# Attention, then two gated matrix layers on one core: spent attention tiles handed to the weights one at a time, a first part in 256 columns, key tiles at the end of the memory, and another issue order

## The chip, the cores and the metric

The kernel runs on one core of one Trainium2 chip. A core has TensorE (PE in the rows; PEld is its weight load), VectorE (DVE), ScalarE (ACT), GpSimd (POOL), SyncE (SP, which here issues every transfer) and 16 DMA engines. The metric is the device time of one execution in microseconds (us), the median of the runs.

## The reference, cut to what matters

```python
# q, k, v: 2 x 8 heads x 768 x 64, float32; scale = 1/8
k_sum = k in blocks of 32 tokens, max;  v_sum = v in blocks of 32, mean   # 24 blocks
scores = concat(scale*q@k.T where |i-j| < 16, scale*q@k_sum.T + log(32))
x = softmax(scores) @ concat(v, v_sum)            # -> 1536 tokens x 512
h = x @ w_in1;  x = (h * clip(h + 3, 0, 6) / 6) @ w_out1   # 512 -> 2048 -> 512
h = x @ w_in2;  x = (h * sigmoid(h)) @ w_out2              # 512 -> 2048 -> 512
```

## The kernel before

**Attention.** 24 units u, each 64 query tokens of one batch with all 8 heads. `load` brings q, k and v in parts of 256 tokens (batch 0's keys, values and first queries into `stage` tiles, the rest into two `qkv` buffers, in two pieces with 64-element runs for q and k), `tr` transposes them on PE (L470), `k_copy`, `q_copy` and `k_max` take them out of PSUM. For a unit come `keys` (POOL), `scores` (PE, L575), `masked` (DVE), `exps` (ACT), `normal` (POOL), `turn` (PE, a transpose, L632), `turned`, and `mix` (PE, L644), whose result `mixed_hi`/`mixed_lo` write as a rounded part and a rest into the input tile x. A mix needs its batch's block sums of v, so all of that batch's v: `v_sums` (PE, L519), `v_add` (DVE) and `v_rows` (PE, L538).

**The layers.** Every operand of a layer is a rounded `float32r` tile (hi) and a rest (lo), and a product is three matmuls (hi·hi, hi·lo, lo·hi). A layer runs in two halves of 8 blocks f of 128 hidden channels, each over three chunks of 512 tokens (tiles x0, x1 and `x_late`). A step i = (layer, half, chunk, f) is `hidden i` (12 matmuls, L682), `act i` (ACT), `gate i` (DVE), `gate_hi i` (ACT or DVE), `gate_lo i` (DVE, L711) and `project i` (12 matmuls in two parts, L732 and L735) into four PSUM banks that a chunk keeps over its 8 steps. There are 96 steps, all 512 columns wide.

**Weights.** 64 pieces h of 512 KB pass through `fetch` (SP), `conv_mag` (ACT), `conv_low`, `conv_clamp`, `conv_join`, `conv_sign` (DVE: rounding to hi), `conv_hi` (DVE or ACT) and `conv_lo` (DVE or POOL, L420). Two pieces fill one weight tile of 8 KB per partition. Eight weight tiles exist at first; four more (`we`), three `gw` and two `rw` tiles come at `end_attention`, when a memory pool with all attention tiles closes; until then there are two `gn` tiles and one `rn`.

**Memory.** Tiles lie behind one another in the order of allocation. Per partition these are: constants 2,144 bytes, x0 and x1 16,384 each, the two key tiles kT (tags ka0, ka1) 12,608 each, and then tiles whose sizes are all multiples of 2,048: `mag`, `bits`, `words`, the weights, the tile `late` (attention's units first, `x_late` afterwards), then the attention pool.

**Order.** `ORDER` is a table written ahead: each engine runs its instructions in that order and waits by semaphores; a star puts an operation on DVE.

Of the kernel before, what the change touches and what calls it, by code (L numbers as in the profile page):

```python
# [78 lines left out]
zero, rouse 0, rouse 1, rouse 2, rouse 3, rouse 4, rouse 5, load k 0 2, table 0, par k 2 1, par k 2 0, tr k 0  # L79
2 0, k_max 0 2 0, k_copy 0 2 0*, tr k 0 2 1, load k 0 0, par k 0 1, par k 0 0, tr k 0 0 1, k_max 0 2 1, k_copy  # L80
0 0 1*, tr k 0 0 0, k_copy 0 0 0*, k_max 0 0 0, load q 0 0, par q 0 0, fetch 0, conv_low 0, par q 0 1, k_copy
0 2 1, clear, tr q 0 0 1, q_copy 0 0 1 1, q_copy 0 0 1 0*, load k 0 1, par k 1 0, conv_mag 0, par k 1 1,
conv_clamp 0, conv_join 0, tr q 0 0 0, q_copy 0 0 0 0, tr k 0 1 1, tr k 0 1 0, k_copy 0 1 0, k_max 0 1 1, load
k 1 1, tr k 1 1 1, k_copy 0 1 1, k_max 0 1 0, k_max 0 0 1, keys 0, k_copy 1 1 1, k_max 1 1 1, keys 3,
conv_sign 0, table 1, tr k 1 1 0, k_max 1 1 0, q_copy 0 0 0 1, scores 0, masked 0, conv_hi 0, exps 0, load k 1
0, tr k 1 0 0, k_max 1 0 0, fetch 1, conv_low 1, conv_mag 1, tr k 1 0 1, keys 1, scores 1, masked 1,
conv_clamp 1, conv_join 1, exps 1, conv_sign 1, guard 0, inverse 0, keys 2, k_copy 1 0 1, guard 1, scores 3,
masked 3, inverse 1, load k 1 2, tr k 1 2 1, tr k 1 2 0, k_max 1 2 0, k_copy 1 0 0, k_copy 1 2 0, load q 0 1,
exps 3, scores 2, masked 2, k_max 1 2 1, guard 3, tr q 0 1 1, q_copy 0 1 1 0, tr q 0 1 0, q_copy 0 1 0 0*,
q_copy 0 1 1 1*, normal 0, turn 0, load v 0 0, normal 1, keys 4, turn 1, k_max 1 0 1, q_copy 0 1 0 1, k_copy 1  # L90
1 0*, v_sums 0 0, v_add 0 0, scores 4, masked 4, keys 7, scores 7, conv_lo 0, exps 2, guard 2, inverse 2,
inverse 3, exps 4, guard 4, conv_hi 1*, load q 0 2, turned 0*, tr q 0 2 0, q_copy 0 2 0 0*, tr q 0 2 1, q_copy
0 2 1 1, q_copy 0 2 0 1, load q 1 0, keys 5, scores 5, inverse 4, tr q 1 0 1, keys 6, turned 1, masked 5, exps
# [824 lines left out]
```

## Time and profile before

| | |
|---|---|
| median of 3 runs | 627.41 us (625.96 to 627.69) |
| the profiled execution, its own time | 626.98 us |
| its span, first to last instruction | 625.2 us |
| granted TensorE clock, mean | 0.989 |
| PE / DVE / ACT / POOL busy, share of the span | 97% / 64% / 39% / 10% |
| last matmul ends | about 622 us |

The span is 1.8 us under that execution's time, and the execution 0.4 us under the median. Matmuls overlap, so PE's busy share says little of its pace; the distance from one matmul's start to the next does.

### The profile page before, as it was taken

The page shows a single profiled execution, that of the slowest core. Times are in us where ns is not written, and L with a number is a line of the kernel's source. Part 1 is how long each engine was busy: PE and PEld are TensorE (multiplying, and loading weights), DVE is VectorE, ACT ScalarE, POOL GpSimd, SP SyncE. Part 2 cuts the span into 40 slices and gives each one's busy share as a digit, 9 for nine tenths or more (in the row PEclk, how much of TensorE's full clock was granted, in tenths as well). Part 3 has the DMA queues.
Part 4 walks back from the last instruction along what each step waited for, and adds up shares of the span by engine and source line. Part 5 has one row for each costly group of instructions (what it writes and reads, how often), then busy time and mean ns, then how long its engine had stood idle before and what let it go on. Part 6 is the DMA issues. An engine that isn't in the chain of part 4 may idle for free.

```text
span 625.2 us, 8645 instructions
## 1 busy us (share of the span) xinstructions
PE 608.6 (97%) x3208; PEld 500.3 (80%) x3208; DVE 398.8 (64%) x908; ACT 243.4 (39%) x568; POOL 63.4 (10%) x90
## 2 busy tenths in 40 slices
PE   6899999999999989999999999999999999999997
PEld 5788788888788868888888888888888888888886
DVE  5789999856569999862369999432159423332442
ACT  3789787454235454331143453211243221111100
POOL 3576443111010000000000000000000000000000
PEclk8799999999999998999999999999999999999999
...
GB/s 240 208 225 179 226 158 141 80 60 26 92 67 135 143 161 136 150 17 1 1 0 102 139 107 128 66 0 1 0 1 101 1 1 1 68 0 1 68 1 67
DMA packets 69051, 51.56 MB, mean 82 GB/s; under 512 B 36369, under 2 KB 63505, under 8 KB 69009
## 3 DMA queue, kind: packets, MB, share of 16 engines
...
q8 instruction: 25, 0.41, 0.3%
...
## 4 chain that ended last, share of the span: by engine, by line
PE 82%; DVE 13%; ACT 3%; issue 1%; POOL 0%; ACTq 0%; DVEq 0%
PE bank L682 37%; PE bank L735 21%; PE bank L732 18%; DVE bits L398 2%; DVE bits L405 2%; PE bank L575 2%; PE bank L644 1%; DVE bits L385 1%; DVE mag L392 1%; PE bank L632 1%; PE bank L470 1%; ACT prob L604 1%; DVE rw L700 1%; DVE gw L711 1%; PE bank L851 1%
## 5 line engine op out<-in xcount | busy, mean ns | idle before, releaser
L682 PE MATMUL bank<-x,w 128*128 128x512 f32 x720 | 179.2, 396 | 0.7 <-DVE x L667 0.7
L682 PEld LDWEIGHTS bank<-x,w 128*128 128x128 f32 x720 | 133.7, 188 | 30.9 <-ACT early_units L604 0.9
L735 PE MATMUL bank<-w,gw 128*128 128x512 f32 (+1 forms) x456 | 103.8, 378 | 0.0
L735 PEld LDWEIGHTS bank<-w,gw 128*128 128x128 f32 x456 | 82.9, 188 | 16.8
L711 DVE TENSOR_TENSOR gw<-rw,gw 128x512 fp32r<-128x512 f32 x80 | 55.1, 689 | 49.2 <-ACT gw L707 47.5
L704 DVE TENSOR_TENSOR rw<-bank,rw 128x512 f32<-128x512 f32 x48 | 32.9, 686 | 69.3 <-ACT rw L695 69.3
L380 ACT ACTIVATE mag<-words 128x512 f32<-128x512 f32 x64 | 43.3, 676 | 65.4 <-DVE bits L398 65.2
L695 ACT ACTIVATE rw<-bank 128x512 f32<-128x512 f32 x48 | 28.4, 595 | 93.6 <-PE bank L682 84.8
L682 PE MATMUL bank<-x,we 128*128 128x512 f32 x240 | 59.0, 393 | 0.0
L732 PE MATMUL bank<-gw,w 128*128 128x512 f32 x240 | 58.0, 390 | 0.0
L707 ACT CAST gw<-rw 128x512 fp32r<-128x512 f32 x45 | 28.0, 622 | 71.1 <-PE bank L735 43.4
L682 PEld LDWEIGHTS bank<-x,we 128*128 128x128 f32 x240 | 45.0, 188 | 10.3
L732 PEld LDWEIGHTS bank<-gw,w 128*128 128x128 f32 x240 | 45.1, 188 | 9.6
L732 PE MATMUL bank<-gn,w 128*128 128x512 f32 x192 | 48.4, 398 | 0.2 <-DVE gn L711 0.2
L398 DVE SCALAR_TENSOR_TENSOR bits<-mag,bits 128x512 uint32<-128x512 uint32 x64 | 45.0, 703 | 0.9
L405 DVE SCALAR_TENSOR_TENSOR bits<-words,bits 128x512 uint32<-128x512 uint32 x64 | 45.0, 703 | 0.4
L732 PEld LDWEIGHTS bank<-gn,w 128*128 128x128 f32 x192 | 35.1, 188 | 8.2 <-DVE gn L711 0.5
L700 DVE SCALAR_TENSOR_TENSOR rw<-rw,bank 128x512 f32<-128x512 f32 x32 | 21.8, 682 | 28.7 <-ACT rw L693 28.7
L732 PE MATMUL bank<-gw,we 128*128 128x512 f32 x144 | 37.6, 406 | 2.4 <-DVE gw L711 0.9
L732 PEld LDWEIGHTS bank<-gw,we 128*128 128x128 f32 x144 | 27.9, 196 | 10.0 <-DVE gw L711 1.7
L735 PE MATMUL bank<-we,gw 128*128 128x512 f32 x144 | 34.7, 390 | 0.0
L682 PE MATMUL bank<-x_late,w 128*128 128x512 f32 x144 | 34.1, 389 | 0.0
...
## 6 DMA issues: line engine op xcount, KB each, us to landing
words<-in_moe_w_in_dram SPq DMA_DIRECT2D x32, 512.0 KB, 3.8
words<-in_moe_w_out_dram SPq DMA_DIRECT2D x32, 512.0 KB, 3.4
...
out_dram<-acc SPq DMA_DIRECT2D x11, 256.0 KB, 2.0
qkv<-in_q_dram SPq DMA_DIRECT2D x10, 256.0 KB, 5.1
stage<-in_k_dram SPq DMA_DIRECT2D x3, 512.0 KB, 5.4
qkv<-in_k_dram SPq DMA_DIRECT2D x6, 256.0 KB, 4.7
stage<-in_v_dram SPq DMA_DIRECT2D x3, 512.0 KB, 6.8
```

What stands on the lines that cost most here:

```text
L380: nc.scalar.activation(out=out, in_=low_high(h)[:, 1].bitcast(F32), func=AF.Abs, scale=EXP_SHIFT)
L398: nc.vector.scalar_tensor_tensor(out=bits, in0=mags.use(h).bitcast(U32), scalar=3, in1=bits, op0=ALU.logical_shift_left, op1=ALU.bitwise_or,)
L405: nc.vector.scalar_tensor_tensor(out=bits, in0=low_high(h)[:, 1], scalar=0x80000000, in1=bits, op0=ALU.bitwise_and, op1=ALU.bitwise_or,)
L575: nc.tensor.matmul(ps[:, hp * NSLOT : (hp + 1) * NSLOT], qT[:, hp, t % 4, :], kw[:, hp, :], start=True, stop=True,)
L682: nc.tensor.matmul(ps, w[:, a, kk * P : (kk + 1) * P], x[:, :, b, kk, :], start=(m == 0), stop=(m == last),)
L695: nc.scalar.activation(out=r, in_=ps, func=AF.Sigmoid)
L700: nc.vector.scalar_tensor_tensor(out=r, in0=r, scalar=6.0, in1=ps, op0=ALU.min, op1=ALU.mult)
L704: nc.vector.tensor_tensor(out=r, in0=ps, in1=r, op=ALU.mult)
L707: copier("gate_hi", i)(out=gs.take(i, 1)[:, 0], in_=rs.use(i))
L711: nc.vector.tensor_tensor(out=g[:, 1], in0=rs.use(i), in1=g[:, 0].bitcast(F32), op=ALU.subtract)
L732: nc.tensor.matmul(ps, lhs, g[:, b], **flags)
L735: nc.tensor.matmul(ps[:, : len(cols)], g[:, a, rows], rhs, **flags)
```

## The change

- The attention pool is gone. Its tiles are named tiles of the one pool under weight tags: the `qkv` buffers in w8, the query tiles in w9 and w10, scores and key windows in w11, pT and vwin in the places of `g2` and `r1`. `grow 0` to `grow 4` turn each into its later use as soon as the table puts it, where `end_attention` did all at once.
- The first part of layer 1 (first chunk, blocks 0 to 3) runs as 8 steps of 256 columns in place of 4 of 512: the first 256 tokens first. So there are 100 steps, and step 28 is what 24 was. Two such steps share a buffer `r` and `g`. `gate_lo` of a 256-column step goes to POOL unless starred (5 of 8 stay on POOL; `gate_lo` 3, 4 and 6 are starred).
- `conv_sign` stands ahead of `conv_clamp` and `conv_join` nearly everywhere.
- kT is allocated last but for small tiles.
- A new `ORDER`, with five `warm` entries (4 matmuls on the identity each). Stars: conv_lo 53 to 26, conv_hi 29 to 24, gate_hi 39 to 57, k_copy 5 to 2, q_copy 8 to 4, mixed_hi 12 to 9, keys 2 to 6.

```diff
-STEPS = [(0, 0, j * WIDE, f) for j in range(NWIDE) for f in range(HALF)]
+FIRST_STEPS = (
+    [(c, 1, f) for c in range(2) for f in range(4)]
+    + [(0, 2, f) for f in range(4, HALF)]
+    + [(c, 2, f) for c in (2, 4) for f in range(HALF)]
+)
+STEPS = [(0, 0, c * SUB, n * SUB, f) for c, n, f in FIRST_STEPS]
...
-    kT = [main.tile([P, NHP * KROW + PAD], F32, tag=f"ka{b}", name=f"kT{b}") for b in range(B)]
...
             nc.tensor.matmul(
-                ps,
+                ps[:, :n],
                 w[:, a, kk * P : (kk + 1) * P],
-                x[:, :, b, kk, :],
+                x[:, o // SUB : (o + n) // SUB, b, kk, :],
...
+    def slot(i):
+
+        n = STEPS[i][3]
+        if n == WIDE:
+            return i, slice(0, WIDE), 1
+        o = i % 2 * SUB
+        return ("pair", i // 2), slice(o, o + SUB), 2
...
     def gate_lo(i):
-        g = gs.see(i)
-        nc.vector.tensor_tensor(
-            out=g[:, 1], in0=rs.use(i), in1=g[:, 0].bitcast(F32), op=ALU.subtract
+        key, cols, _ = slot(i)
+        r, g = rs.use(key), gs.see(key)
+        eng = nc.vector if STEPS[i][3] == WIDE or ("gate_lo", i) in ON_DVE else nc.gpsimd
+        eng.tensor_tensor(
+            out=g[:, 1, cols], in0=r[:, cols], in1=g[:, 0, cols].bitcast(F32), op=ALU.subtract
         )
...
-    raws = ring(apool, "qkv", 2, [P, 2 * DM])
-    gs = ring(apool, "gn", LAG, [P, 2, WIDE], F32R)
-    rs = ring(apool, "rn", 1, [P, WIDE])
-    qTs = ring(apool, "qT", 2, [P, NHP, 4, 2 * QW])
-    sts = ring(apool, "stat", 4, [P, 3, NHP])
+
+    def plain(tag):
+        return main.tile([P, 2048], F32, tag=tag, name=f"early_{tag}")
+
+    raw = plain("w8")
+    raws = Ring([raw[:, : 2 * DM], raw[:, 2 * DM :]])
+    qTs = Ring(
+        [plain(tag).rearrange("p (h w t) -> p h w t", h=NHP, w=4) for tag in ("w9", "w10")]
+    )
+    gs = ring(main, "g", LAG, [P, 2, WIDE], F32R)
+    rs = ring(main, "r", 1, [P, WIDE])
...
+    kT = [main.tile([P, NHP * KROW + PAD], F32, tag=f"ka{b}", name=f"kT{b}") for b in range(B)]
...
-    def end_attention():
-        att.close()
-        pool = ctx.enter_context(tc.tile_pool(name="wextra", bufs=1))
-        ws.free += ring(pool, "we", EXTRA, [P, 2, 1024], F32R).free
-        assert not gs.held and not rs.held
-        gs.free = ring(pool, "gw", LAG + 1, [P, 2, WIDE], F32R).free
-        rs.free = ring(pool, "rw", 2, [P, WIDE]).free
+    def grow(n):
+
+        if n < 4:
+            if n == 0:
+                assert not raws.held
+            elif n < 3:
+                assert len(qTs.held) == 2 - n
+            add_weights([HALF + n])
+        else:
+            gs.free.append(main.tile([P, 2, WIDE], F32R, tag="g2", name="g2"))
+            late_r = main.tile([P, 2 * WIDE], F32, tag="r1", name="r1")
+            rs.free += [late_r[:, :WIDE], late_r[:, WIDE:]]
```

How the order moves, at three places. On PE at the first hidden step, before (L470 is `tr`, L644 `mix`, L632 `turn`, L575 `scores`, L682 `hidden`; a row's x counts instructions, and a plain float32 matmul stands twice in the trace):

```order
L644 MATMUL bank_81<-early_units 64x64 x8
L644 MATMUL bank_78<-pT_109,vwin_111 64x64 x8
L632 MATMUL bank_74<-cst,prob_107 120x128 x4
L470 MATMUL bank_77<-cst,qkv_93 128x128 x4
L644 MATMUL bank_79<-early_units 64x64 x8
L644 MATMUL bank_81<-pT_110,vwin_112 64x64 x8
L632 MATMUL bank_74<-cst,prob_108 120x128 x4
L575 MATMUL bank_78<-kw_106,qT_99 128x120 x4
L682 MATMUL bank_79<-x_0_64,w_90 128x512 x12
```

The same place of the changed kernel (L649 is `mix`, L637 `turn`, L580 `scores`, L688 `hidden`, L475 `tr`):

```order
L649 MATMUL bank_74<-early_g_96,early_r_97 64x64 x8
L580 MATMUL bank_72<-early_w_95,early_w_90 128x120 x4
L475 MATMUL bank_73<-cst,early_w_88 128x128 x4
L475 MATMUL bank_79<-cst,early_w_88 128x128 x4
L637 MATMUL bank_75<-cst,early_w_95 120x128 x4
L649 MATMUL bank_78<-early_g_96,early_r_97 64x64 x8
L580 MATMUL bank_74<-early_w_95,early_w_90 128x120 x4
L580 MATMUL bank_77<-early_units,early_w_90 128x120 x4
L649 MATMUL bank_73<-early_units 64x64 x8
L649 MATMUL bank_78<-early_units 64x64 x8
L637 MATMUL bank_79<-cst,early_units 120x128 x4
L688 MATMUL bank_73<-x_0_64,w_85 128x256 x12
```

The first hidden step now stands behind 4 mixes instead of 8, 12 scores instead of 16, 18 `tr` instead of 22 and 7 turns instead of 10.

On SP, the loads up to batch 0's last v, before (L428 and L443 are attention's loads, L372 `fetch`, L835 constants):

```order
L443 DMA qkv_94<-in_k_dram 128x8x64 x2
L372 DMA words_72<-in_moe_w_out_dram 128x1024
L443 DMA qkv_93<-in_k_dram 128x8x64 x2
L443 DMA qkv_94<-in_q_dram 128x8x64 x2
L428 DMA stage_89<-in_v_dram 128x8x128
L443 DMA qkv_93<-in_q_dram 128x8x64 x2
L443 DMA qkv_94<-in_q_dram 128x8x64 x2
L428 DMA stage_89<-in_v_dram 128x8x128
L428 DMA stage_85<-in_v_dram 128x8x128
```

And in the changed kernel (L433 and L448 are the loads, L377 `fetch`, L874 constants):

```order
L448 DMA early_w_88<-in_k_dram 128x8x64 x2
L874 DMA cst<-in_consts_dram 128x360
L377 DMA words_71<-in_moe_w_in_dram 128x4x256
L448 DMA early_w_88<-in_q_dram 128x8x64 x2
L377 DMA words_69<-in_moe_w_out_dram 128x1024
L433 DMA stage_84<-in_v_dram 128x8x128
L433 DMA early_w_88<-in_v_dram 128x8x128
L433 DMA stage_84<-in_v_dram 128x8x128
L433 DMA stage_80<-in_v_dram 128x8x128
```

In both tables 15 loads of 512 KB and the two of constants end with that v; 6 of the 15 came in two pieces of short runs (x2), now 3 do, and 4 weight pieces stand ahead instead of 2.

On DVE, at the gate of step 24 and the next steps, the first ones of layer 1's second half, before (L385, L398, L405, L392 are the rounding, L420 `conv_lo`, L700 `gate`, L711 `gate_lo`):

```order
L700 SCALAR_TENSOR_TENSOR rw_1793<-rw_1793,bank_80 128x512
L420 TENSOR_TENSOR w_90<-bits_70,w_90 128x512
L392 TENSOR_SCALAR mag_68<-mag_68 128x512
L385 TENSOR_SCALAR bits_70<-words_73 128x512
L398 SCALAR_TENSOR_TENSOR bits_69<-mag_68,bits_69 128x512
L711 TENSOR_TENSOR gw_1791<-rw_1793,gw_1791 128x512
L405 SCALAR_TENSOR_TENSOR bits_69<-words_71,bits_69 128x512
L392 TENSOR_SCALAR mag_68<-mag_68 128x512
L700 SCALAR_TENSOR_TENSOR rw_1792<-rw_1792,bank_74 128x512
```

And at the same computation in the changed kernel, the gate of step 28 (L722 `gate`, L730 `gate_hi`, L736 `gate_lo`, L390, L397, L403, L410 the rounding):

```order
L403 SCALAR_TENSOR_TENSOR bits_67<-mag_66,bits_67 128x512
L421 CAST w_86<-bits_67 128x512
L722 SCALAR_TENSOR_TENSOR r_93<-r_93,bank_78 128x512
L730 CAST g_1909<-r_93 128x512
L736 TENSOR_TENSOR g_1909<-r_93,g_1909 128x512
L722 SCALAR_TENSOR_TENSOR r_1910<-r_1910,bank_79 128x512
L736 TENSOR_TENSOR g_92<-r_1910,g_92 128x512
L410 SCALAR_TENSOR_TENSOR bits_68<-words_71,bits_68 128x512
L397 TENSOR_SCALAR mag_66<-mag_66 128x512
```

The gate's three operations stand together now, where four or more operations of the weights' rounding stood among them. In the whole table ahead of that step's projection DVE had 35 `conv_low`, 34 `conv_join` and 22 `conv_lo`; now it has 31, 30 and 14.

## Rows read from the trace of the kernel before

**Rows 1.** The page, busy time, share of the span, instructions.

```profile
PE 608.6 (97%) x3208; PEld 500.3 (80%) x3208; DVE 398.8 (64%) x908; ACT 243.4 (39%) x568; POOL 63.4 (10%) x90
```

**Rows 2.** Windows: length, busy time of each engine, granted clock, DMA share, GB/s.

```profile
31.30:46.90 15.60, 14.18 (x170) 12.58 (x171) 13.79 (x70) 13.10 (x53) 10.95 (x21) 1.00 0.97 225
62.50:94.00 31.50, 31.25 (x232) 24.42 (x231) 29.81 (x78) 24.21 (x71) 14.87 (x13) 1.00 0.71 193
188.00:229.00 41.00, 41.00 (x181) 33.69 (x180) 40.90 (x82) 20.88 (x37) 0.00 (x0) 1.00 0.47 143
229.00:238.20 9.20, 6.83 (x20) 4.32 (x19) 9.00 (x18) 4.12 (x9) 0.00 (x0) 0.81 0.53 166
281.00:312.00 31.00, 31.00 (x136) 25.36 (x136) 8.77 (x15) 4.64 (x8) 0.00 (x0) 1.00 0.01 1
```

**Rows 3.** PE's timeline up to the first hidden step: start, us, idle before.

```profile
36.49 0.60 PE L470 MATMUL bank<-cst,qkv 128*128 128x128 f32 x4
36.93 1.05 PE L575 MATMUL bank<-kw,qT 128*128 128x120 f32 x8
37.81 0.60 PE L632 MATMUL bank<-cst,prob 128*120 128x128 f32 x4
38.98 1.22 PE L519 MATMUL bank<-stage,cst 128*32 128x128 f32 x32
...
55.17 0.69 PE L644 MATMUL bank<-early_units 120*64 120x64 f32 x16
55.68 0.64 PE L644 MATMUL bank<-pT,vwin 120*64 120x64 f32 x16
...
58.79 3.07 PE L682 MATMUL bank<-x,w 128*128 128x512 f32 x12 [0.71 <-DVE x L667]
```

**Rows 4.** PE's timeline around 229 us.

```profile
229.00 0.39 PE L732 MATMUL bank<-gw,we 128*128 128x512 f32 x1
229.61 0.73 PE L732 MATMUL bank<-gw,we 128*128 128x512 f32 x2 [0.22 <-DVE gw L711]
231.14 0.96 PE L732 MATMUL bank<-gw,we 128*128 128x512 f32 x3 [0.80 <-DVE rw L700]
232.75 0.49 PE L732 MATMUL bank<-gw,we 128*128 128x512 f32 x1 [0.65 <-DVE gw L707]
233.96 4.37 PE L732 MATMUL bank<-gw,we 128*128 128x512 f32 x11 [0.71 <-DVE gw L711]
238.16 1.55 PE L732 MATMUL bank<-gw,w 128*128 128x512 f32 x6
```

**Rows 5.** PE's timeline in two long runs of hidden steps, with the next row.

```profile
177.01 16.48 PE L682 MATMUL bank<-x_late,w 128*128 128x512 f32 x72
193.34 2.88 PE L732 MATMUL bank<-gw,w 128*128 128x512 f32 x12
...
404.61 8.55 PE L682 MATMUL bank<-x,w 128*128 128x512 f32 x36
413.00 1.54 PE L735 MATMUL bank<-w,gw 128*128 128x512 f32 x6
```

**Rows 6.** Groups by line, PE, 619.2 to 622.1 us: count, busy us, mean ns.

```profile
L735 PE MATMUL bank<-w,gw 128*128 128x256 f32 x12 | 1.6, 282 | 0.0
```

**Rows 7.** Groups by line, whole span: DVE's and POOL's conv_lo.

```profile
L420 DVE TENSOR_TENSOR w<-bits,w 128x512 fp32r<-128x512 f32 x38 | 26.1, 690 | 0.1
L420 POOL TENSOR_TENSOR w<-bits,w 128x512 fp32r<-128x512 f32 x10 | 13.7, 1367 | 24.3 <-ACT w L416 16.6 <-DVE stat L619 5.9 <-DVE w L416 1.8
```

**Rows 8.** Timelines of POOL and DVE, 53 to 62 us.

```profile
53.42 0.99 POOL L624 TENSOR_TENSOR prob<-prob,stat 128x480 f32<-128x480 f32 x1 [0.77 <-DVE stat L619]
...
53.43 1.26 DVE L392 TENSOR_SCALAR mag<-mag 128x512 f32<-128x512 f32 x1
...
61.57 0.41 DVE L392 TENSOR_SCALAR mag<-mag 128x512 f32<-128x512 f32 x1
```

**Rows 9.** DMA issues: count, KB each, median us to landing.

```profile
words<-in_moe_w_out_dram SPq DMA_DIRECT2D x32, 512.0 KB, 3.4
qkv<-in_q_dram SPq DMA_DIRECT2D x10, 256.0 KB, 5.1
```

More of the change, by code (lines that the diff above doesn't have):

```diff
@@ L78 @@
 ORDER = """
[L79 to L93, printed above, removed]
@@ new lines @@
+scores 10, load_v 2, mix 2, conv_mag 4, conv_clamp 4, load_v 3, mixed_hi 2, mixed_lo 2, unstage, normal 7, mix
+3, mixed_hi 3, mixed_lo 3, turn 7, turned 7, normal 6, turn 6, conv_hi 3, conv_lo 3, turned 6, conv_join 4,
+conv_hi 4, load q 1 0, hidden 0 0, hidden 0 1, act 0, masked 9, tr q 1 0 1, masked 10, q_copy 1 0 1 0, q_copy
+1 0 1 1*, tr q 1 0 0, q_copy 1 0 0 1, fetch 5, conv_mag 5, hidden 1 0, hidden 1 1, conv_lo 4*, hidden 2 0,
+q_copy 1 0 0 0, act 1, gate 0, gate_hi 0, load q 1 2, tr q 1 2 1, conv_low 5, conv_sign 5, q_copy 1 2 1 0,
@@ new lines @@
+gate 1, gate_hi 1, conv_clamp 5, conv_join 5, keys 13, scores 13, q_copy 1 2 1 1, normal 4, turn 4, tr q 1 2
+0, turned 4, fetch 6, conv_low 6, conv_mag 6, keys 12, q_copy 1 2 0 0, conv_sign 6, q_copy 1 2 0 1, conv_clamp
+6, conv_join 6, conv_hi 5, masked 11, gate_lo 0, gate_lo 1, conv_hi 6, hidden 2 1, conv_lo 6, project 0 0,
+project 1 0, load_v 4, mix 4, mixed_hi 4, mixed_lo 4, act 2, load_v 6, mix 6, gate 2, mixed_hi 6, mixed_lo 6,
+load_v 5, mix 5, masked 8, mixed_hi 5, mixed_lo 5, exps 9, guard 9, load_v 7, mix 7, hidden 3 0, hidden 3 1,
@@ new lines @@
+8, conv_sign 8, exps 13, guard 13, mixed_hi 9*, mixed_lo 9, conv_join 8, inverse 13, act 4, gate 4, fetch 11,
+gate_hi 4*, gate_lo 4*, normal 8, turn 8, gate_lo 5, project 5 0, exps 11, guard 11, project 5 1, conv_hi 8*,
+turned 8, act 6, gate 6, gate_hi 6, gate_lo 6*, load v 1 1, v_pair 1 1, v_sums 1 1, normal 13, turn 13, turned
+13*, hidden 7 0, hidden 7 1, act 7, gate 7, gate_hi 7, scores 12, masked 12, fetch 9, conv_mag 9, conv_low 9,
+conv_sign 9, exps 12, project 4 0, conv_clamp 9, guard 12, scores 15, fetch 10, masked 15, exps 15, conv_lo 8,
@@ new lines @@
+0 0 0 0, conv_mag 16, normal 16, turn 16, normal 17, fetch 21, fetch 18, keys 21, turned 16, scores 18, load_v
+16, gate_hi 12*, gate_lo 12, conv_clamp 16, act 13, turn 17, conv_join 16, masked 19, conv_hi 16, project 12
+0, hidden 14 0, hidden 14 1, masked 18, exps 18, guard 18, inverse 18, gate 13, gate_hi 13*, gate_lo 13, mix
+16, turned 17, mix 17, finish 0 0 0 3, exps 19, conv_low 17, guard 19, inverse 19, mixed_hi 17, conv_sign 17,
+normal 18, turn 18, mixed_lo 17, mixed_hi 16, project 13 0, conv_lo 16*, act 14, project 12 1, turned 18,
@@ new lines @@
+mixed_lo 16, hidden 15 0, hidden 15 1, conv_mag 17, keys 20*, normal 19, gate 14, conv_clamp 17, turn 19,
+gate_hi 14, gate_lo 14, project 14 0, conv_join 17, scores 20, masked 20, scores 21, conv_hi 17, project 14 1,
+conv_lo 17, conv_mag 18, conv_clamp 18, act 15, gate 15, keys 23*, conv_low 18, conv_sign 18, gate_hi 15*,
+grow 1, gate_lo 15, turned 19, masked 21, project 13 1, load_v 19, exps 21, guard 21, keys 22, scores 22,
+conv_join 18, hidden 16 0, conv_hi 18*, hidden 16 1, act 16, fetch 19, gate 16, inverse 21, normal 21*,
@@ L724, in products @@
             banks.take((chunk, m), 1)
-        ps, w, g = banks.see((chunk, m)), ws.see((layer * 2 + half) * HALF + f), gs.see(i)
+        ps, w, g = banks.see((chunk, m)), ws.see((layer * 2 + half) * HALF + f), gs.see(slot(i)[0])
+        shift = slot(i)[1].start
         if layer:
```

423 lines of the change are left out of this document (215 added, 208 removed).

## The prediction

> **What bounds the kernel now.** I read the page's busy times first. PE is busy 97% of the span [rows 1], so the question is not which engine to relieve but at what places PE is idle or goes at less than its best pace. The windows show three kinds of stretch [rows 2]. Up to about 60 us PE waits for attention: the DMA engines are full (0.97 in 31.3 to 46.9 us) and DVE and ACT nearly so. From 62 to 125 us PE has no gaps worth naming, but DVE is at its limit (29.81 of 31.50 us), so a little more work on DVE there would show. From 188 to 238 us DVE is full again (40.90 of 41.00, then 9.00 of 9.20 us), and there alone, after attention, PE stops: 6.83 of 9.20 us busy, with the granted clock at 0.81 on the mean, that is, some of it at the lower level, after PE had been idle four times. Later DVE has room in plenty (8.77 of 31.00 us) and PE sets the pace.
>
> Then I read PE's timeline for the pace, from one row's start to the next. A run of 72 hidden matmuls on `x_late` goes from 177.01 to 193.34 us, which is 226.8 ns each; a run of 36 on x0 or x1 goes from 404.61 to 413.00 us, 233.1 ns each [rows 5]. It is the same instruction with the same shape, in stretches where nobody makes PE wait. So there is a third cost, small per matmul, that no idle time shows.
>
> **The stall at 229 us.** Between 229.00 and 238.16 us PE ran 18 matmuls [rows 4]. At 226.8 ns they take 4.08 us, so 5.08 us were lost, to idle time and to the lower clock after it. Each wait ends at a gate operation on DVE. The gate was late because DVE was full of rounding for weights that were not wanted yet: in the order rows, rounding stands between `gate`, `gate_hi` and `gate_lo`. I added up, by the mean durations of each kind, what the table puts ahead of that projection: some 204 us of DVE work against 201 us of PE work before, some 193 us against 213 us now. The difference comes from four fewer pieces rounded, eight fewer `conv_lo` on DVE at 0.69 us [rows 7], and more PE work put ahead. PE also starts behind by what it idled early; DVE idled early as well, so I compare the sums alone. With some 20 us of room where there was none, I take the whole 5.1 us back; the bounds are 5.1 and nothing. The work that hides the rounding afterwards is the projections of layer 1's second half, where DVE is free most of the time; if they did not hide it, the stall would come back as the next late gate.
>
> **The pace on x0 and x1.** Why is it slower? The weight load runs beside the matmul, so two streams read the memory at once. Everything that PE reads in a layer except x0 and x1 lies behind the two key tiles, whose 2 x 12,608 bytes are 49 x 512 + 128 bytes. All other sizes there are multiples of 2,048. So before, x0 and x1 stand 128 bytes off the weights, counted modulo 512, while `x_late`, g and the weights stand at the same offset to each other. With the key tiles last, all of them stand at the same offset. If it is the distance between the two streams that matters, the pitch becomes 226.8 ns for all hidden matmuls: 64 of the layer steps use x0 or x1, 64 x 12 = 768 matmuls, at 6.3 ns, 4.8 us less. The bounds are 4.8 us gained, nothing, and (below) a loss; I take the gain, because every pair of equal offsets in the trace is fast and every unequal one slow. The Trainium skill speaks against it (TensorE: Matmul & The Clock Gate, Step-by-step: what each phase is for): TensorE reads SBUF through two independent ports, one for the moving operand and one for the weights. By that rule the two addresses could not meet, x0 and x1, which stay where they are, would stay slow, and the sum would be 4.8 us higher. The rows show the two paces but not which of the two readings holds.
>
> **256 columns.** Eight steps of 256 columns replace four of 512: 192 matmuls for 96. In the last microseconds 12 of 256 columns are busy 1.6 us, the last with its 0.282 us; 1.318 us over 11 starts is 0.120 us each [rows 6]. So 192 x 0.120 = 23.0 us for 96 x 0.2268 = 21.8 us: 1.3 us more. There the weight load belongs to g, not w, but the shape is the same. The bound below is nothing (half of 226.8 each), above some 3 us.
>
> **The start.** Less stands ahead of the first hidden step now: 4 scores at 0.88, 4 `tr` and 3 turns at 0.44, 4 mixes at 0.51 us [rows 3], together 8.6 us, against 0.2 us more for sums. Five `warm` entries cost some 2 us but stand where PE waits for data, so I count them at nothing; without that cover they cost their 2 us. So if the first hidden step starts at 58.8 - 8.4 = 50.4 us, the start is neither better nor worse. When does it start? The sums over the last v ran on PE at 38.98 us, with the DMA engines full. Ahead of that load stand 15 loads now as before, but three fewer in two pieces. A piece of 256 KB takes 5.1 us to land, a weight piece of 512 KB 3.4 us [rows 9], so I put that moment at 37 to 40 us. From there to the last `mixed_lo` that the first step needs, the new table has about 12 us of DVE work (two `masked`, four k_max, eight `mixed` operations, a rounding among it), and DVE works without pause there in the trace of before. That gives 50 to 52.5 us; I take 51.4, so 1.0 us lost. The bounds are 3 us gained (v early, DVE instructions overlapping by their usual 0.08 us) and 5 us lost.
>
> **At nothing.** `conv_sign` ahead of `conv_join` is the same work; it lets go of a `words` tile earlier, and after 125 us the fetches are not what anything waits for. Handing over tiles one at a time adds no instructions; its use is counted in the stall. Five `gate_lo` on POOL take some 0.7 us each, by half of the 1.37 us of a 512-column subtraction [rows 7], in place of 0.4 on DVE; other PE work stands between them and their projections. The end of the program has the same rows.
>
> **Sum**, on the profiled execution: 626.98 - 5.1 - 4.8 + 1.3 + 1.0 = 619.4 us. The median is 0.4 us above that execution, so 619.8 us.
>
> **Rivals.**
> 1. *The pace stays slow on x0 and x1*, because it is a matter of these tiles and not of the distance to the weights: 624.6 us. For it: both have stayed at their address. Against: nothing in their own form differs from `x_late`.
> 2. *The start gets worse*: DVE is the limit up to 125 us, and POOL can hold it up. An operation of DVE that began 0.01 us after one of POOL took 1.26 us, where the same takes 0.41 us otherwise [rows 8]: 0.85 us. That is a rule of the Trainium skill, too (SBUF — State Buffer, Who interferes with whom): an instruction of GpSimd and one of VectorE that uses their shared port exclude each other for the whole instruction, whichever is first; the trace agrees. `conv_lo` on POOL rises from 11 to 38. If the new ones fell into the full stretch, each could cost 0.85 us; but up to the end of the first chunk the table has about as many there as before, and only the five `gate_lo` are new. They are in the chain that PE waits for: 5 x 0.85 = 4.3 us, and with a first step 2 us later some 6 us: 625.8 us.
> 3. *The stall moves* instead of going: the four new tiles become free at four moments, and one comes late for its weights. The price is the same 5.1 us: 624.9 us.
> 4. *Slower: the offset itself is what is slow*, not the distance. Then the 1,536 matmuls that were fast before (384 hidden, 1,152 projections) stand at the slow offset, too. At 6.3 ns they cost 9.7 us, and x0 and x1 win nothing: 619.8 + 4.8 + 9.7 = 634.3 us. It decides if the runs on `x_late` show 233 ns. Against it: an absolute offset would have to matter while the fast one is no rounder than the slow one (both are 32 modulo 64).
>
> **How the numbers follow.** The forecast has 0.52 (its own range 615 to 624 us, by the bounds of the start and the 256 columns), rival 1 has 0.15, rival 2 0.13, rival 3 0.11, rival 4 0.09. About 0.3%, 1.9 us, is what a measurement can tell from no change: faster is under 625.5, slower over 629.3 us. All of the forecast, 0.10 of rival 1, 0.05 of rival 2 and 0.06 of rival 3 lie on the faster side: 0.73. Slower are rival 4 and 0.03 of rivals 2 and 3: 0.12. The same has 0.15. The range is 614 to 629 us; it leaves out rival 4 and the outer parts of the others.
>
> **What would show it.** Right, if long runs of hidden matmuls on x0 and x1 show 226 to 228 ns; if PE has no idle time over 0.3 us after attention and the clock stays at its upper level there; if a 256-column matmul goes at 0.12 us; and if the first one starts at 50 to 53 us. Wrong, if runs on `x_late` go at 233 ns, if PE waits for `gate_lo` on POOL before 80 us, or if DVE is full where the first projections of the second half stand.

## The result

The changed kernel takes 620.62 us (median of 4 runs, 619.35 to 622.03) against 627.37 us before (625.96 to 627.69): a ratio of 0.9897, with a 95% interval of 0.9871 to 0.9923. The forecast was 619.8 us. The profiled execution of the changed kernel is the longest of its four, 622.03 us with a span of 620.2 us; the sum of the prediction for it was 619.4 us. So 5.0 of the 7.6 us of the sum are in that trace, 6.7 in the medians.

The page of the changed kernel, busy time and share of the span, answers to [rows 1]: PE's share stays at 97% of a shorter span, and POOL has more to do, 38 `conv_lo` for 11 among it (10 of the 11 are in [rows 7]). DVE's total has not fallen (406.8 us for 398.8), so what counts for the stall is where its work stands.

```profile
PE 603.6 (97%) x3324; PEld 506.6 (82%) x3324; DVE 406.8 (66%) x895; ACT 240.3 (39%) x574; POOL 100.4 (16%) x113
```

The windows of the changed kernel, with the columns of [rows 2] and three of its stretches:

```profile
62.50:94.00 31.50, 30.14 (x320) 27.72 (x316) 29.55 (x102) 24.83 (x92) 19.41 (x19) 1.00 0.68 167
188.00:229.00 41.00, 41.00 (x182) 33.98 (x181) 29.50 (x54) 12.75 (x22) 4.83 (x4) 1.00 0.28 89
229.00:238.20 9.20, 9.20 (x42) 7.61 (x42) 5.85 (x12) 4.17 (x8) 1.91 (x2) 1.00 0.20 57
```

DVE was full from 188 to 229 us (40.90 of 41.00) and has 29.50 us of work there now. PE, which stopped after 229 us before, is busy 9.20 of 9.20 us, and the clock stays at its upper level (1.00). The stall is gone, and PE's list of waits has none after 80 us.

PE's timeline of the changed kernel, two runs of hidden matmuls with the row behind each, answers to [rows 5]:

```profile
208.41 5.60 PE L688 MATMUL bank<-x_late,w 128*128 128x512 f32 x24
213.85 2.88 PE L759 MATMUL bank<-g,w 128*128 128x512 f32 x12
...
412.47 5.60 PE L688 MATMUL bank<-x,w 128*128 128x512 f32 x24
417.91 1.30 PE L762 MATMUL bank<-w,g 128*128 128x512 f32 x5
```

Both runs take 5.44 us for 24 matmuls, 226.7 ns each. The 233.1 ns on x0 and x1 are gone, and `x_late` has kept its pace.

The start in PE's timeline of the changed kernel answers to [rows 3]; every row up to 125 us in which PE waited after the first hidden step is among these, and so are two runs of 256 columns:

```profile
52.37 1.81 PE L688 MATMUL bank<-x,w 128*128 128x256 f32 x12
...
57.06 0.73 PE L688 MATMUL bank<-x,w 128*128 128x256 f32 x4 [0.32 <-DVE w L425]
...
63.64 0.69 PE L649 MATMUL bank<-early_g,early_r 120*64 120x64 f32 x16 [0.42 <-DVE stat L595]
64.52 0.69 PE L649 MATMUL bank<-early_units 120*64 120x64 f32 x16 [0.19 <-DVE x L672]
...
66.67 1.60 PE L759 MATMUL bank<-g,w 128*128 128x256 f32 x12
68.11 3.04 PE L688 MATMUL bank<-x,w 128*128 128x256 f32 x24
70.99 0.60 PE L637 MATMUL bank<-cst,early_w 128*120 128x128 f32 x4
...
79.67 0.65 PE L637 MATMUL bank<-cst,early_w 128*120 128x128 f32 x4 [0.76 <-POOL early_w L629]
```

The first hidden step starts at 52.37 us, inside the 50 to 52.5 us of the forecast. Twelve projections of 256 columns take 1.44 us and 24 hidden matmuls 2.88 us: 0.120 us each, as reckoned. Not reckoned were the four waits, 1.69 us together. Before there was one of 0.22 us in the same part of the program, in the profiled execution; the other kernels with that start wait 0.21 (e2) to 1.75 us (e3) for DVE there.

### The profile page after: what moved, and what is told of

It reads as the page before. It is cut to its first block, busy times and chain, and to the rows that moved or that the text cites. A ratio compares the mean times of both kernels' runs of the same rounds, so it can differ in the third digit from the quotient of the medians.

```text
span 620.2 us, 8857 instructions
## 1 busy us (share of the span) xinstructions
PE 603.6 (97%) x3324; PEld 506.6 (82%) x3324; DVE 406.8 (66%) x895; ACT 240.3 (39%) x574; POOL 100.4 (16%) x113
## 4 chain that ended last, share of the span: by engine, by line
PE 90%; DVE 4%; ACT 3%; DMA 1%; issue 1%; SPq 0%; POOL 0%; ACTq 0%; POOLq 0%
PE bank L688 41%; PE bank L762 21%; PE bank L759 20%; PE bank L580 3%; PE bank L649 2%; PE bank L637 2%; DMA stage<-in_q_dram 1%; ACT early_w L508 1%; DVE bits L410 1%; DVE bits L403 1%; ACT kT L483 1%; ACT early_w L609 0%; PE bank L524 0%; PE bank L475 0%; DVE bits L390 0%
## 5 line engine op out<-in xcount | busy, mean ns | idle before, releaser
L688 PE MATMUL bank<-x,w 128*128 128x512 f32 (+1 forms) x1008 | 231.3, 381 | 0.4 <-DVE w L425 0.3
L688 PEld LDWEIGHTS bank<-x,w 128*128 128x128 f32 x1008 | 182.6, 188 | 36.3 <-DVE w L425 0.5
L759 PE MATMUL bank<-g,w 128*128 128x512 f32 (+1 forms) x624 | 141.3, 376 | 0.0
L762 PE MATMUL bank<-w,g 128*128 128x512 f32 (+1 forms) x600 | 135.7, 381 | 0.0
L762 PEld LDWEIGHTS bank<-w,g 128*128 128x128 f32 x600 | 109.6, 188 | 21.8
L759 PEld LDWEIGHTS bank<-g,w 128*128 128x128 f32 x624 | 110.3, 188 | 20.7 <-DVE g L736 0.2
L425 POOL TENSOR_TENSOR w<-bits,w 128x512 fp32r<-128x512 f32 x38 | 51.0, 1347 | 353.5 <-ACT w L421 196.7
L736 DVE TENSOR_TENSOR g<-r,g 128x512 fp32r<-128x512 f32 (+1 forms) x95 | 66.9, 709 | 29.2 <-ACT g L730 26.3
L385 ACT ACTIVATE mag<-words 128x512 f32<-128x512 f32 x64 | 43.0, 671 | 27.6 <-DVE bits L403 20.1
L722 DVE SCALAR_TENSOR_TENSOR r<-r,bank 128x512 f32<-128x512 f32 (+1 forms) x52 | 33.1, 641 | 27.6 <-ACT r L714 27.1
L410 DVE SCALAR_TENSOR_TENSOR bits<-words,bits 128x512 uint32<-128x512 uint32 x64 | 48.5, 758 | 1.3
L403 DVE SCALAR_TENSOR_TENSOR bits<-mag,bits 128x512 uint32<-128x512 uint32 x64 | 47.2, 737 | 1.6
L688 PE MATMUL bank<-x_late,w 128*128 128x512 f32 x192 | 44.8, 389 | 0.0
L688 PEld LDWEIGHTS bank<-x_late,w 128*128 128x128 f32 x192 | 36.0, 188 | 7.5
L730 ACT CAST g<-r 128x512 fp32r<-128x512 f32 (+1 forms) x43 | 25.4, 594 | 36.0 <-PE bank L762 16.4
L397 DVE TENSOR_SCALAR mag<-mag 128x512 f32<-128x512 f32 x64 | 31.6, 493 | 9.0 <-ACT mag L385 8.8
L730 DVE CAST g<-r 128x512 fp32r<-128x512 f32 (+1 forms) x57 | 28.8, 505 | 11.9 <-PE bank L762 8.3
```

The lines of the kernel that those rows point to most:

```text
L385: nc.scalar.activation(out=out, in_=low_high(h)[:, 1].bitcast(F32), func=AF.Abs, scale=EXP_SHIFT)
L397: nc.vector.tensor_scalar(out=mag, in0=mag, scalar1=MAG_MIN, scalar2=MAG_MAX, op0=ALU.max, op1=ALU.min)
L403: nc.vector.scalar_tensor_tensor(out=bits, in0=mags.use(h).bitcast(U32), scalar=3, in1=bits, op0=ALU.logical_shift_left, op1=ALU.bitwise_or,)
L410: nc.vector.scalar_tensor_tensor(out=bits, in0=low_high(h)[:, 1], scalar=0x80000000, in1=bits, op0=ALU.bitwise_and, op1=ALU.bitwise_or,)
L425: eng.tensor_tensor(out=w_half(h, 1), in0=bitss.use(h).bitcast(F32), in1=w_half(h, 0).bitcast(F32), op=ALU.subtract,)
L688: nc.tensor.matmul(ps[:, :n], w[:, a, kk * P : (kk + 1) * P], x[:, o // SUB : (o + n) // SUB, b, kk, :], start=(m == 0), stop=(m == last),)
```

## The experiments

Two theories had to be told apart from their rivals: that the distance between the two streams sets the pace on x0 and x1, and that the stall at 229 us came from a DVE that was full of rounding. All ratios are to the kernel before on the same chip.

### The pace alone (e1)

The key tiles move behind `late`. Two small shifts put the attention pool and the later weight pool, which follow them, at the same offset as the rest:

```diff
-    kT = [main.tile([P, NHP * KROW + PAD], F32, tag=f"ka{b}", name=f"kT{b}") for b in range(B)]
...
+    kmax = [apool.tile([P, NHP, NB], F32, tag="kmax0", name="kmax0")]
     raws = ring(apool, "qkv", 2, [P, 2 * DM])
...
     late = main.tile([P, 2 * KD * WIDE], F32, tag="late", name="early_units")
+    kT = [main.tile([P, NHP * KROW + PAD], F32, tag=f"ka{b}", name=f"kT{b}") for b in range(B)]
...
+        pool.tile([P, 96], F32, tag="gap", name="gap")
         ws.free += ring(pool, "we", EXTRA, [P, 2, 1024], F32R).free
```

> The kernel before, with the key tiles moved behind the other tiles and two small shifts, so that x0, x1, x_late, every weight tile and every gate tile stand at the same offset modulo 512 bytes; no instruction is moved. If the distance between the two streams sets the pace: long runs of hidden matmuls on x0 and x1 go from 233 to 227 ns, the stall at 229 us stays, and the time falls by 4.8 us to 622.6 us. If the pace belongs to the tiles x0 and x1 (which keep their addresses): 233 ns and 627.4 us, no change.

Measured: 622.85 us, ratio 0.9929 (0.9902 to 0.9956). PE's timeline of this kernel, the same kind of run as in [rows 5]:

```profile
401.52 8.32 PE L681 MATMUL bank<-x,w 128*128 128x512 f32 x36
409.69 1.52 PE L734 MATMUL bank<-w,gw 128*128 128x512 f32 x6
```

It is 8.17 us for 36, 226.9 ns, where it was 233.1. No instruction was moved and x0 and x1 kept their addresses. The stall stayed. The first theory holds, to within half a microsecond.

### The distance put back into the changed kernel (e4, e12)

Two (e4) or four (e12) of the `stat` tiles of 64 bytes go between x1 and what lies behind it. In e4:

```diff
     x1 = [main.tile(x_shape, F32R, tag=f"x{j}", name=f"x1_{j}") for j in range(NWIDE - 1)]
+    sts = [main.tile([P, 3, NHP], F32, tag=f"stat{i}", name=f"stat{i}") for i in range(2)]
...
-    sts = ring(main, "stat", 4, [P, 3, NHP])
+    sts = Ring(sts + [main.tile([P, 3, NHP], F32, tag=f"stat{i}", name=f"stat{i}") for i in range(2, 4)])
```

> The changed kernel with two of its small stat tiles (64 bytes each) put between x1 and everything behind it: x0 and x1 keep their addresses and the key tiles stay last, but the weights stand 128 bytes off again, modulo 512. If the distance sets the pace: hidden matmuls on x0 and x1 at 233 ns, those on x_late at 227 ns, and 620.6 + 4.8 = 625.4 us. If it is the order of the tiles or the absolute place of x0 and x1: 227 ns everywhere and 620.6 us.

> As e4 with four stat tiles in place of two: x0 and x1 stand 256 bytes from the weights, modulo 512. If every distance other than a multiple of 512 is slow: 233 ns on x0 and x1, 625.4 us. If the pattern repeats every 256 bytes: 227 ns and 620.6 us.

Measured: e4 625.49 us, ratio 0.9973 (0.9957 to 0.9989), 4.9 us over the changed kernel. e12 620.31 us, ratio 0.9883 (0.9866 to 0.9900), the same as the changed kernel. PE's timelines, first of e4, then of e12:

```profile
316.50 13.76 PE L689 MATMUL bank<-x_late,w 128*128 128x512 f32 x60
330.10 2.20 PE L760 MATMUL bank<-g,w 128*128 128x512 f32 x9
...
394.75 8.55 PE L689 MATMUL bank<-x,w 128*128 128x512 f32 x36
403.14 1.54 PE L763 MATMUL bank<-w,g 128*128 128x512 f32 x6
```

```profile
390.81 8.32 PE L689 MATMUL bank<-x,w 128*128 128x512 f32 x36
398.97 1.30 PE L763 MATMUL bank<-w,g 128*128 128x512 f32 x5
```

With 128 bytes between them the run on x0 or x1 is back at 8.39 us for 36, 233.1 ns, while `x_late`, which moved along with the weights, has 226.7 ns. With 256 bytes it is 226.7 ns. So the distance matters, and 256 is as good as 512: only the "modulo 512" of the prediction was too strict. All that lies behind x1 moved together; that the weights are what counts in it is argued, from the two tiles that such a matmul reads, x and w.

### Less on DVE, more on POOL (e2, e3)

Eight `conv_lo` of the kernel before lose their star and go to POOL; e3 has the edit of e1 as well.

```diff
-hidden 17 1, conv_hi 20*, conv_clamp 21, conv_lo 20*, hidden 19 0, conv_join 21, act 17, conv_low 22, conv_mag
+hidden 17 1, conv_hi 20*, conv_clamp 21, conv_lo 20, hidden 19 0, conv_join 21, act 17, conv_low 22, conv_mag
...
```

> The kernel before, with eight conv_lo (20 to 27, all in 188 to 229 us) taken from DVE to POOL, which is idle there; nothing else is moved. If the stall at 229 us comes from a full DVE: 8 x 0.69 = 5.5 us less on DVE, the 5.1 us of the stall go to nearly nothing, and the time falls to 622.3 to 623 us. If POOL holds DVE up for as long as it works, or if the gates wait for something else than DVE's queue: the stall stays and the time is 627.4 us or more.

> Both edits of the two runs before together, on the kernel before with its own order of work and no step of 256 columns. If pace and stall are two separate costs: 627.4 - 4.8 - 5.1 = 617.5 us, which would be some 3 us under the changed kernel, and that difference would be what its steps of 256 columns and its new start cost. If a faster pace only moves the stall (PE reaches the late gates sooner): some 620 to 622 us, with a stall of 3 to 5 us left near 225 us.

Measured: e2 631.05 us, ratio 1.0053 (1.0030 to 1.0076): worse. e3 626.35 us, ratio 0.9987 (0.9970 to 1.0003), 3.5 us worse than e1, as e2 is 3.8 us worse than the kernel before. The timelines of POOL and DVE in e2 show why:

```profile
202.88 1.48 POOL L420 TENSOR_TENSOR we<-bits,we 128x512 fp32r<-128x512 f32 x1 [3.49 <-ACT we L416]
203.11 1.52 DVE L707 CAST gw<-rw 128x512 fp32r<-128x512 f32 x1
...
205.97 1.37 POOL L420 TENSOR_TENSOR w<-bits,w 128x512 fp32r<-128x512 f32 x1 [1.61 <-ACT w L416]
206.42 0.69 DVE L700 SCALAR_TENSOR_TENSOR rw<-rw,bank 128x512 f32<-128x512 f32 x1 [0.25 <-ACT rw L693]
207.03 0.59 DVE L385 TENSOR_SCALAR bits<-words 128x512 uint32<-128x512 uint32 x1
```

The CAST takes 1.52 us where it has 0.42 otherwise: it ends only when POOL has done. `gate` at 206.42 us, which reads PSUM, has its usual 0.69 us; the TENSOR_SCALAR behind it waits for POOL's end again. I compared each DVE operation from 188 to 229 us with the mean of its kind in the kernel before: they are longer by 7.3 us together, against 8 x 0.69 = 5.5 us saved. DVE ended with some 2 us more to do, not 5.5 less. That rival won, and the run is no test of a relieved DVE; it shows that a DVE with more to do makes a longer stall. That an operation of POOL and one of DVE exclude each other for the whole instruction is the rule of the Trainium skill that the prediction used in its rival 2 (SBUF — State Buffer, Who interferes with whom); the trace agrees, and `gate`, which takes one of its operands from PSUM, is not held up.

### Less on DVE, more on ACT (e5)

On the kernel of e1, four `conv_hi` and three `gate_hi` lose their stars and go to ACT:

```diff
-hidden 17 1, conv_hi 20*, conv_clamp 21, conv_lo 20*, hidden 19 0, conv_join 21, act 17, conv_low 22, conv_mag
+hidden 17 1, conv_hi 20, conv_clamp 21, conv_lo 20*, hidden 19 0, conv_join 21, act 17, conv_low 22, conv_mag
...
```

> The kernel before with its offsets made equal (as in e1, 622.85 us), and now four conv_hi (20, 22, 27, 28) and three gate_hi (18, 19, 23) go from DVE to ACT, which is busy 20.9 of 41 us ahead of the stall: 7 x 0.42 = 2.9 us less on DVE, none of it on POOL. If a full DVE makes the stall near 229 us, and e2 was worse only because POOL held DVE up: the stall shrinks by about 2.9 us and the time is 619.9 to 620.5 us. If the gates wait for something else: 622.9 us.

Measured: 621.16 us, ratio 0.9891 (0.9862 to 0.9921), beside 0.9929 (0.9902 to 0.9956) of e1: the intervals overlap. PE's timelines, first of e1, then of e5:

```profile
228.97 0.39 PE L731 MATMUL bank<-gw,we 128*128 128x512 f32 x1
229.89 0.73 PE L731 MATMUL bank<-gw,we 128*128 128x512 f32 x2 [0.53 <-DVE gw L710]
231.43 0.98 PE L731 MATMUL bank<-gw,we 128*128 128x512 f32 x3 [0.80 <-DVE rw L699]
...
236.88 1.52 PE L731 MATMUL bank<-gw,w 128*128 128x512 f32 x6
```

```profile
228.96 0.86 PE L731 MATMUL bank<-gw,we 128*128 128x512 f32 x3
230.60 0.96 PE L731 MATMUL bank<-gw,we 128*128 128x512 f32 x3 [0.79 <-DVE rw L699]
...
236.04 1.52 PE L731 MATMUL bank<-gw,w 128*128 128x512 f32 x6
```

The 18 matmuls of [rows 4] take 7.91 us in e1 and 7.08 in e5 (4.08 us at their pace). One wait of 0.53 us went, the others stayed: of 2.9 us taken from DVE, 0.8 us came out at the stall. Right in its direction, not in its size. As a kernel it is not told apart from the changed one (620.62 us, 0.9897): with the order of work of before, moving the key tiles and seven operations gave what the whole change gave.

### Gates ahead of rounding (e9, e11)

On the kernel of e1 again, the rest of gate 24 and `gate 25` move ahead of the rounding in DVE's queue. `gate_hi 25` and `gate_lo 25` move forward, too, but in e9 they still stand behind rounding of pieces 31 and 32. In e9 (the entries as they stand in the order, the moved ones marked):

```diff
 project 21 1,
+gate_hi 24, gate_lo 24, act 25, gate 25,
 conv_sign 31, conv_clamp 32, conv_hi 31, fetch 34, conv_join 32, project 22 0,
-gate_hi 24,
 conv_lo 31*, conv_mag 33,
-gate_lo 24,
 hidden 27 0, conv_sign 32,
-act 25,
 conv_clamp 33, conv_hi 32, fetch 35,
-gate 25,
 project 22 1,
+gate_hi 25*, gate_lo 25, act 26, gate 26,
 conv_lo 32*, conv_low 33, project 23 0, conv_low 34,
-gate_hi 25*,
...
```

In e11 `project 22 0`, `hidden 27 0`, `project 22 1`, `gate_hi 25*` and `gate_lo 25` stand right behind `gate 25`, and the rounding from `conv_sign 31` on behind them; `act 26` and `gate 26` are at their old place.

> The kernel of e1 (before with equal offsets, 622.85 us) with eight entries of its order moved, none added or taken away: gate_hi 24, gate_lo 24, act 25 and gate 25 stand right behind project 21 1, and gate_hi 25, gate_lo 25, act 26 and gate 26 right behind project 22 1, each ahead of the rounding that stood before them. If the stall near 229 us is gates queued behind rounding that is not wanted yet: it goes nearly whole, with the lower clock after it, and the time is 618 to 619.5 us. If DVE is short of time as a whole there: the rounding is late instead, the stall moves to the next projections or hidden steps, and the time stays at 622 to 623 us.

> As e9, but with gate_hi 25 and gate_lo 25 right behind gate 25, so that the rounding of pieces 31 and 32 (conv_sign, conv_clamp, conv_join, conv_lo: some 3.2 us of DVE) stands behind both gates; in e9 it stood ahead of gate_hi 25, for which PE waited 1.77 us, and 11 matmuls after it went at 0.37 us in place of 0.227. If only the order on DVE made the stall: PE waits nowhere from 200 to 260 us, the clock stays up, and the time is 617.5 to 618.5 us, under the changed kernel's 620.6. If DVE is short of time as a whole: another gate or weight is late in its place and the time is 621 to 623 us.

Measured: e9 621.97 us, ratio 0.9928 (0.9904 to 0.9952), no better than e1. e11 623.39 us, ratio 0.9937 (0.9916 to 0.9959), no better either. PE's timelines, first of e9, then of e11, and of e11 the row of ACT that PE waits for first:

```profile
225.60 1.52 PE L731 MATMUL bank<-gw,we 128*128 128x512 f32 x6
228.90 0.49 PE L731 MATMUL bank<-gw,we 128*128 128x512 f32 x1 [1.77 <-DVE gw L706]
229.63 4.28 PE L731 MATMUL bank<-gw,we 128*128 128x512 f32 x11 [0.23 <-DVE gw L710]
233.74 1.55 PE L731 MATMUL bank<-gw,w 128*128 128x512 f32 x6
```

```profile
226.83 2.88 PE L731 MATMUL bank<-gw,we 128*128 128x512 f32 x12
231.86 2.23 PE L731 MATMUL bank<-gw,we 128*128 128x512 f32 x6 [2.15 <-ACT acc L774]
...
238.98 3.02 PE L681 MATMUL bank<-x,w 128*128 128x512 f32 x12 [1.14 <-ACT acc L774]
```

```profile
228.43 0.63 ACT L415 CAST w<-bits 128x512 fp32r<-128x512 f32 x1 [2.72 <-DVE bits L404]
...
231.22 1.08 ACT L774 ACTIVATE acc<-bank 128x512 f32<-128x512 f32 x2
```

In e9 gate 24 is in time, and `gate_hi 25` is the late one: between it and `gate 25` DVE has six operations of rounding, from 225.22 to 228.42 us. The 18 matmuls take 8.14 us, 11 of them 0.374 us each, and the mean granted clock from 226 to 234 us is 0.79. The profiled execution of e9 (619.26 us) is 2.7 us under its median because its first hidden step came at 55.73 us, in e1's profile at 58.06; from that step to the end e9 takes 561.8 us and e1 562.0.

In e11 both gates are in time and the first 12 matmuls run through: so the rounding ahead of the gates did make them late. But the wait is at the next thing. PE needs a bank that `finish` on ACT has not emptied, since `finish` stands behind a `conv_hi` that waited 2.72 us for the rounding that I had moved back. That fits the second theory of both expectations, a DVE short of time as a whole (40.90 of 41.00 us), where another order of the same work only moves the wait. It is not shown: an order with `finish` ahead of `conv_hi` as well wasn't tried, and PE's timeline of e11 has no wait for a weight up to 300 us.

### How much room the new order has (e6, e7)

The changed kernel with `conv_clamp` of pieces 21 to 29 done four or eight times:

```diff
         mag = mags.see(h)
-        nc.vector.tensor_scalar(
-            out=mag, in0=mag, scalar1=MAG_MIN, scalar2=MAG_MAX, op0=ALU.max, op1=ALU.min
-        )
+        for _ in range(4 if 21 <= h <= 29 else 1):
+            nc.vector.tensor_scalar(
+                out=mag, in0=mag, scalar1=MAG_MIN, scalar2=MAG_MAX, op0=ALU.max, op1=ALU.min
+            )
```

> The changed kernel, with conv_clamp of the nine pieces 21 to 29 done four times instead of once (the result is the same): 27 x 0.42 = 11.3 us more on DVE between the last tile handed over and the first projection of layer 0's second half, columns 512 and up. If the new order left DVE some 20 us of room there: no change, 620.6 us. If the stall was only just avoided: some 11 us more, up to 632 us. If DVE was never the limit: no change here and in the next run.

> As the run before, with conv_clamp of those nine pieces done eight times: 63 x 0.42 = 26.5 us more on DVE. If there were some 20 us of room (DVE is idle 17.5 us from 196 to 260 us): the stall is back, with 6 to 10 us, and the time is 627 to 631 us. If DVE was never the limit: 620.6 us.

Measured: e6 631.38 us, ratio 1.0069 (1.0046 to 1.0091); e7 648.42 us, ratio 1.0340 (1.0313 to 1.0368). That is 10.8 us more for 11.3 us of DVE work, and 27.8 for 26.5: nearly all of it, then more than all. There is no room of 20 us. The changed kernel's own timelines of DVE, POOL and PE at `project 20`, the first one that e6 makes late, say the same:

```profile
192.98 0.69 DVE L722 SCALAR_TENSOR_TENSOR r<-r,bank 128x512 f32<-128x512 f32 x1 [1.44 <-ACT r L714]
193.70 1.11 DVE L730 CAST g<-r 128x512 fp32r<-128x512 f32 x1
194.85 0.69 DVE L736 TENSOR_TENSOR g<-r,g 128x512 fp32r<-128x512 f32 x1
```

```profile
191.99 2.55 POOL L425 TENSOR_TENSOR w<-bits,w 128x512 fp32r<-128x512 f32 x2 [4.28 <-issue]
```

```profile
196.17 5.60 PE L759 MATMUL bank<-g,w 128*128 128x512 f32 x24
```

`gate_hi 20` ends at 194.81 us and `gate_lo 20` at 195.54, and the projection starts at 196.17: 1.4 and 0.6 us ahead. DVE's idle time before `gate 20` (1.44 us) is a wait for `act 20`. That stands on ACT behind a `conv_hi`, which had itself waited 2.28 us for DVE's rounding; so more rounding ahead of the gate moves all of it back, and in e6 that idle time is still 1.33 us. The CAST of `gate_hi 20` takes 1.11 us where it has 0.42 otherwise: two `conv_lo` on POOL run up to 194.54 us beside it. So the subtractions on POOL took 0.69 us from the margin at this gate. In e6 PE waits 2.73 us at that place, for `gate_hi`:

```profile
197.55 0.47 PE L760 MATMUL bank<-g,w 128*128 128x512 f32 x1 [2.73 <-DVE g L731]
```

### gate_lo of 256 columns on DVE (e8)

```diff
-6, conv_join 6, conv_hi 5, masked 11, gate_lo 0, gate_lo 1, conv_hi 6, hidden 2 1, conv_lo 6, project 0 0,
+6, conv_join 6, conv_hi 5, masked 11, gate_lo 0*, gate_lo 1*, conv_hi 6, hidden 2 1, conv_lo 6, project 0 0,
...
```

> The changed kernel with the five gate_lo of 256 columns that POOL does (steps 0, 1, 2, 5, 7) given to DVE. If they cost nothing on POOL, as the forecast has it: 620.6 us. If POOL's work holds DVE up in the stretch up to 85 us and PE waits for it (rival 2): up to 4 us less, 616.5 to 618.5 us. If DVE is so full there that 5 x 0.41 us more is what shows: 621 to 623 us.

Measured: 630.2 us, ratio 1.0053 (1.0034 to 1.0073): 9.6 us worse than the changed kernel, more than any of the three had it. In PE's timeline of this kernel three projections wait:

```profile
62.53 2.72 PE L759 MATMUL bank<-g,w 128*128 128x256 f32 x11 [2.64 <-DVE g L736]
...
83.85 1.57 PE L759 MATMUL bank<-g,w 128*128 128x256 f32 x11 [2.92 <-DVE g L736]
...
95.63 1.10 PE L759 MATMUL bank<-g,w 128*128 128x256 f32 x5 [2.00 <-DVE g L736]
```

They are 7.56 us together, and the mean granted clock from 50 to 100 us is 0.90, where the changed kernel has 1.00.

On POOL, `gate_lo 0` of the changed kernel starts at 57.98 us and goes past what stands ahead of it on DVE; on DVE both first ones come at 62.05 us, behind the rounding and eight rows of `masked`:

```profile
57.98 1.13 POOL L736 TENSOR_TENSOR g<-r,g 128x256 fp32r<-128x256 f32 x1 [0.84 <-ACT g L730]
```

```profile
62.05 0.75 DVE L736 TENSOR_TENSOR g<-r,g 128x256 fp32r<-128x256 f32 x2
```

So it isn't the 0.41 us of the operation that counts, but the queue in which it stands. Yet on POOL these operations are not free either. Beside `gate_lo 1` a rounding operation of DVE takes 1.22 us where it has 0.69 otherwise (POOL, then DVE, in the changed kernel):

```profile
59.37 0.73 POOL L736 TENSOR_TENSOR g<-r,g 128x256 fp32r<-128x256 f32 x1 [0.26 <-ACT g L730]
```

```profile
59.43 1.22 DVE L403 SCALAR_TENSOR_TENSOR bits<-mag,bits 128x512 uint32<-128x512 uint32 x1
```

DVE goes on from there without a pause to the `masked` for which PE waits 0.42 us at 63.64 us.

### Without warm (e10)

```diff
-0, conv_lo 0*, load k 0 2, par k 2 0, par k 2 1, fetch 1, conv_low 1, conv_mag 1, conv_clamp 1, warm 1, load q
+0, conv_lo 0*, load k 0 2, par k 2 0, par k 2 1, fetch 1, conv_low 1, conv_mag 1, conv_clamp 1, load q
...
```

> The changed kernel without its five warm entries (ten matmuls of 128 columns in fp32 on the constants, of whose result nothing is used). If they stand where PE waits anyway, as the forecast has it: 620.6 us, within 1 us. If they are on the path: some 2 us less, 618.5 us. If they keep TensorE's clock at its upper level in the first 60 us and that is worth something: 622 us or more, with a lower granted clock there.

Measured: 620.56 us, ratio 0.9909 (0.9883 to 0.9936): no change. The windows of e10 and of the changed kernel have a granted clock of 0.91 and 0.94 up to 60 us, and the first hidden step starts at 50.90 us in e10. An entry is two matmul instructions, so the five are ten (20 rows of the trace). They stand where PE waits anyway.

## Why the prediction was right

**The stall: right in its size, wrong in its reason's number.** 5.1 us were reckoned; in the trace the stall is gone whole, and the clock with it stays up. (In e1 the same stall lost 3.83 us, without the lower clock, so a part of the 5.1 belongs to that one execution.) But the step "some 20 us of room where there was none" failed. It set sums of DVE and PE work against each other, and e6 and e7 show that added work comes out nearly whole in the time: the gates of `project 20` are 1.4 and 0.6 us ahead of PE, not 20. That so little was enough for the whole stall to go is luck as far as the sum is concerned. What the sum left out is that DVE works in its order: its idle time lies where it waits for ACT or for PE, and where ACT in turn waits for the rounding, more rounding does not go into it. It also left out that POOL's subtractions would lengthen a gate operation (0.69 us at `gate_hi 20`). That DVE was the bound in the kernel before is borne out by its 40.90 of 41.00 us, by e2 (more for DVE, a longer stall) and weakly by e5. That rounding ahead of the gates made them late, as the prediction had put it, e11 bears out; but moving it back only moved the wait, and whether that is because DVE was short of time over the whole stretch, or because `finish` then stood badly on ACT, stays open. Which part of the change cleared it, the tiles handed over one by one or the new order, isn't told apart: neither was run without the other.

**The pace: right, by the mechanism and the number.** 4.8 us were reckoned; e1 alone gives 4.4 us, e4 takes 4.9 us back. Rival 1 (it belongs to x0 and x1) and rival 4 (the offset itself is slow) are out: x0 and x1 kept their addresses in all three kernels, and `x_late` and the weights moved by 128 bytes, modulo 512, and are fast at either place. The Trainium skill's two independent read ports (TensorE: Matmul & The Clock Gate, Step-by-step: what each phase is for) do not describe this. The measurement decides, and by it the pace does depend on the distance between the two; by what mechanism is not shown.

**256 columns: right.** 0.120 us a matmul in the trace, so the 1.3 us for the eight steps stand as reckoned.

**The start: the first step right, the waits behind it left out.** The sum was 2.6 us too low for the profiled execution. The first hidden step came at 52.37 us where 51.4 was reckoned, 1.0 us of the 2.6; the four small waits before 80 us are 1.5 us more than in the profile of the kernel before, and were reckoned at nothing. They come again, 1.68 to 1.80 us together, in e4, e6, e7, e10 and e12. In the profiles of the other kernels with this start (e10 without `warm`) the first hidden step comes at 50.87 to 52.31 us (e4, e6, e7, e8, e10, e12), so 51.4 is where it usually is, and the start moves by 1.5 us between executions. That is what separates 622.03 us from the median: from the first hidden step to the end of the span the changed kernel takes 567.8 us, and e10 and e12, with 620.56 and 620.77 us, take 567.9. (By the same measure e4 takes 572.6 us, e6 577.3 and e8 578.5.) In the seven profiles with the start of before the step comes at 55.66 to 59.68 us, so the 58.79 us from which the prediction reckoned is one draw from a wide range, and the 1.0 us lost rests on it.

**At nothing.** `warm` costs nothing (e10). No PE wait ends at a `gate_lo` on POOL, and e8 gives what they would cost on DVE; but they lengthened DVE's work ahead of a `masked` that PE waited for, so nothing is a little too low. Rival 2's lock between POOL and DVE is there (e2: 1.1 us on one CAST). It is in the changed kernel, too: `conv_lo` on POOL lengthens a DVE operation of the layers' gates or the rounding at 186.54, 193.70, 243.80 and 247.57 us by 0.7 to 1.1 us each. PE waits for none of them. `conv_sign` ahead of `conv_join` was not tried alone.

**Rival 3** (the stall moves) didn't come true in the changed kernel, where PE waits nowhere after 80 us, but e11 shows the like: the wait went to another place.
